# Cross-attention reads and a max-of-three FFN: eight single PSUM banks, turned scores for two batches, and a new order

## The chip, the cores and the metric

The kernel runs on one core of one Trainium2 chip. The metric is device time in microseconds (us), the median of the runs. The engines are TensorE (PE, with its weight loads PEld), VectorE (DVE), ScalarE (ACT), GpSimd (POOL) and SyncE (SP); each works through its own queue in order.

## The reference

`x` is 8 x 8 x 512 x 64 (batch, head, token, depth), `state` 8 x 8 x 32 x 64. Both read each other by attention, and the result goes, per token, through a network whose hidden layer is the largest of three products.

```python
scores = scale * np.matmul(x, state.transpose(0, 1, 3, 2))
a = np.exp(scores - scores.max(-1, keepdims=True)); a /= a.sum(-1, keepdims=True) + 1e-09
xread = np.matmul(a, state)
scores2 = scale * np.matmul(state, x.transpose(0, 1, 3, 2))
a2 = np.exp(scores2 - scores2.max(-1, keepdims=True)); a2 /= a2.sum(-1, keepdims=True) + 1e-09
sread = np.matmul(a2, x)
x = np.concatenate([xread, sread], axis=2)      # then (B*S', H*D) = 4352 x 512
h = np.maximum(np.maximum(x @ w1, x @ w2), x @ w3)
out = h @ w_out                                  # 512 -> 768 -> 512
```

## The kernel before

The exponentials are taken without subtracting the maximum; the sums are looked at near the end, and a branch repeats the work with the maximum if they are out of bounds (it is not taken here). `xread` is never formed: since `xread @ w` is `a @ (state @ w)`, the kernel computes G = state x w for each batch and uses it as the weights of layer 1.

Work is written as a list of short steps, `PLAN`, and each engine's queue holds its instructions in the order of that list; no scheduler moves them. Two further tables give each step its PSUM bank (`BANKS`, and `PAIRS` for tiles of two banks) and its SBUF buffer (`PLACES`). The steps, with b a batch and m one of six blocks of 128 hidden columns:

- `lst`, `lxu`, `lxg`, `lx`, `lw`, `lwo`: loads of state, x, the three weights and w_out. `clr`, `ident`, `zero`, `warm`: constants. `busy`: a PE product nobody uses, which keeps PE working while it waits for data.
- `stc`, `stt`, `stp` k: states of batches 2k and 2k+1 are cast, turned on PE (L261) and placed in a block-diagonal tile `bd`. `xt`/`xtc`: x is turned on PE and copied out (batches 0, 1); `xtd`: turned by DMA from SP.
- `sc` b (PE, L305): scores, x being the standing operand and `bd` the moving one; `ex` (ACT, L313): exponentials e; `sum` (DVE, L342): their sums and reciprocals; `wt` (POOL or DVE, L349): a = e / sum; `at`/`atc` (PE and a copy) or `atd` (DMA from SP): aT. Letters at the end of a step name the engine: A, D, P, S.
- `pad` (POOL, L375): x with a column of ones, so that `sr` (PE, L391) gives the second read with its sum; `srs`, `srt`, `ap` scale it, turn it by DMA and place it. Batches 0 and 1 have no padded x: their `sr` reads 64 columns of x and 64 ones.
- `g` b m, `gr`, `gq` b c0 c1 (PE, L427): G, on eight 64x32 tiles of the array at once; `gc`, `grc`, `gqc` copy it out of PSUM (L444, L466, L469).
- `l1` b m (PE, L477): three products of 512 columns with two passes each, into three banks; `m0` (ACT, L492), `ma`, `mb` (DVE, L497, L505): the largest of the three, ht. `l1s` m: the same for the second reads of all batches. `l2` b j, `l2p` (PE, L514, L532), `l2c`, `l2pc`, `so`, `sop`: layer 2, copies and stores.
- `hold`: one last PE product and a DVE copy of it, ahead of the branch.

Before, PSUM is four single banks and two pairs. A pair takes the G products of both head parities or the scores of a batch, and one instruction then copies both banks:

```python
p = open_ps["g", b, m] = two_banks([128, 2, 512], F32, "pg")
...
copier[c[g]](out=G[b][:, g:h, :, m * 128:m * 128 + 128], in_=p[:, g:h, 0:384]...)
```

The plan begins with batches 0 and 1 together; from batch 2 on each batch repeats one pattern.

Of the kernel before, what the change touches and what calls it, by code (L numbers as in the profile page):

```python
# [18 lines left out]
    lst 0 A; lxu 0 0 S; zero; clr 0; clr 1; clr 2; clr 3; warm; lxg 0 1; busy 1; xones 1; ident; busy 1;  # L19
    lxg 1 0; busy 1; busy 1; stc 0 D; busy 1; busy 1; busy 1; busy 1; busy 1; lxg 1 1; stt 0; busy 1; busy 1;  # L20
    cxu 0 0 D; xt 0 0; stp 0 A; busy 1; xt 0 1; lw 0 2 1; lw 0 1 0; xtc 0 0 D; sc 0 0; xones 0; lw 0 2 2;
    xtc 0 1 D; busy 1; busy 1; sc 0 1; xt 1 0; ex 0 0; ex 0 1; lw 1 3 0; sum 0 0; sum 0 1; xtc 1 0 A; busy 1;
    busy 1; xt 1 1; sc 1 0; xtc 1 1 D; ex 1 0; busy 1; busy 1; sc 1 1; lw 2 3 2; wt 0 1 D; lw 2 3 1; lw 3 4 0;
    wt 0 0 P; lw 3 6 2; at 0 0; sr 0; ex 1 1; sr 1; g 0 0; sum 1 0; wt 1 0 P; g 1 0; atc 0 0 A; at 0 1; at 1 0;
    gc 0 0 A; atc 0 1 A; g 1 1; sum 1 1; gc 1 0 D; atc 1 0 A; srs 0; srs 1; g 0 1; wt 1 1 P; at 1 1; gc 0 1 A;
    l1 0 0; atc 1 1 D; lst 1 A; m0 0 0; lst 3 A; gc 1 1 A; ma 0 0; lw 3 6 1; lw 4 6 0; lxg 2 1; lxg 2 0; l1 0 1;
    m0 0 1; lwo; mb 0 0; g 0 2; g 1 2; ma 0 1; l1 1 0; lst 2 A; gc 0 2 A; mb 0 1; m0 1 0; ma 1 0; l1 0 2;
    mb 1 0; gc 1 2 A; m0 0 2; ma 0 2; l1 1 1; m0 1 1; g 1 3; stc 1 P; mb 0 2; ma 1 1; g 0 3; mb 1 1; stt 1;
    gc 1 3 A; l1 1 2; gc 0 3 A; m0 1 2; stp 1 DA; ma 1 2; g 0 4; g 0 5; l1 0 3; gc 0 5 D; g 1 4; mb 1 2;
    gc 0 4 A; m0 0 3; gc 1 4 A; ma 0 3; gr 2 1792 2304; mb 0 3; l1 1 3; m0 1 3; grc 2 1792 2304 A; xtd 2;  # L30
    ma 1 3; l1 0 5; stc 2 P; g 1 5; gr 2 0 512; mb 1 3; m0 0 5; ma 0 5; l1 1 4; gc 1 5 A; gr 2 1280 1792;
    m0 1 4; grc 2 0 512 D; mb 0 5; gr 2 512 1024; ma 1 4; grc 2 1280 1792 AD; l1 0 4; m0 0 4; ma 0 4; stt 2;
# [45 lines left out]
BANKS = """  # L78
    0123012301 2230210020 1121020310 2321302130 1203102301 2310213012 3120132132 3102301230 2301203103 2103120132
    1032103210 3213201321 0312013201 3201320120 3120132103 1203120312 0310321031 2013210321 0321032132 0132103120  # L80
    1320132103 2103120120 1201320123 0123120123 0213012013 0130123102 2
"""
PAIRS = """
    0101010101 1001010010 0110101010 1010101010 10
"""
PLACES = """
# [657 lines left out]
```

## Time and profile before

| | us |
|---|---|
| median of 3 runs (152.44 to 152.64) | 152.61 |
| span of the profiled execution, first to last instruction | 150.5 |
| median less span | 2.1 |
| PE busy | 145.1 |
| DVE busy | 118.0 |
| ACT busy | 83.2 |
| POOL busy | 56.1 |

The profile is of one execution. The page gives its span; its whole time is not on the page, so the 2.1 us are the distance from the span to the median of the timed runs. "busy" counts instructions of an engine; matmuls are pipelined, so their durations overlap, and the time a group takes on PE is read from the chain in order of time, not from the mean of one.

### The profile page before, as it was taken

What the parts mean: (1) busy time and instruction counts of PE and PEld (TensorE: products, weight loads), DVE (VectorE), ACT (ScalarE), POOL (GpSimd) and SP (SyncE); (2) the same over time, 40 slices, a digit from 0 to 9 for tenths busy, and PEclk for the clock granted to TensorE, in tenths of its full rate; (3) what the DMA queues carried; (4) which work ended last, traced back from release to release, by engine and by line L of the source; (5) the groups of instructions that cost most, each with busy time, mean ns of one, the idle gap of its engine ahead of it and who ended that gap; (6) DMA issues with size and microseconds to landing.
All of it is one profiled execution on the core that took longest, in us unless ns stands there. A gap on an engine that the chain in (4) does not pass through costs nothing.

```text
span 150.5 us, 3618 instructions
## 1 busy us (share of the span) xinstructions
PE 145.1 (96%) x1422; PEld 72.8 (48%) x1422; DVE 118.0 (78%) x202; ACT 83.2 (55%) x144; POOL 56.1 (37%) x78
## 2 busy tenths in 40 slices
PE   6998999999999999999999999999999999999991
PEld 2556443335444443444344434443444446689770
DVE  6488788999967899789978997899789888674443
ACT  3366888965654574457546764676466653332220
POOL 6996911090392507350735064506250200001500
PEclk9999999999999999999999999999999999999999
DMA  4999999949647996998399839983303340300555
GB/s 121 195 188 189 206 230 198 196 97 139 124 97 171 235 182 189 108 209 178 145 102 216 183 139 90 231 183 131 157 4 78 121 175 7 139 0 17 190 199 167
DMA packets 39108, 22.29 MB, mean 148 GB/s; under 512 B 23072, under 2 KB 36896, under 8 KB 39088
## 3 DMA queue, kind: packets, MB, share of 16 engines
q0 software_dynamic: 15872, 13.96, 49.3%
q1 hardware_dynamic: 21632, 6.69, 22.8%
q10 hardware_dynamic: 1584, 1.38, 3.2%
q8 instruction: 12, 0.20, 0.6%
q14 instruction: 8, 0.07, 0.2%
HBM read 15.20 MB, written 8.91 MB: 160 GB/s over the span
## 4 chain that ended last, share of the span: by engine, by line
PE 88%; DMA 5%; POOL 3%; issue 1%; DVE 1%; ACT 1%; POOLq 0%
PE pw L477 47%; PE po L514 25%; PE pg L427 6%; DMA w<-in_moe_w_dram 5%; PE po L532 4%; PE ps L305 2%; PE psr L391 2%; POOL w L217 1%; POOL x L206 1%; PE pgh L427 1%; ACT G L444 1%; PE pt L261 1%; DVE held L593 0%; PE idle L591 0%; PE pat L358 0%
## 5 line engine op out<-in xcount | busy, mean ns | idle before, releaser
L477 PE MATMUL pw<-aT,G 128*128 128x512 bf16 x288 | 66.7, 379 | 0.0
L492 ACT CAST t<-pw 128x512 bf16<-128x512 f32 (+1 forms) x54 | 30.5, 564 | 27.3 <-PE pw L477 26.4
L497 DVE TENSOR_TENSOR t<-t,pw 128x512 bf16<-128x512 bf16 (+1 forms) x54 | 35.3, 654 | 11.1 <-ACT t L492 8.9
L477 PEld LDWEIGHTS <-G 128*128 128x128 bf16 x288 | 27.1, 98 | 32.8 <-issue 2.1
L514 PE MATMUL po<-wout,ht 128*128 128x512 bf16 x168 | 39.7, 379 | 0.0
L505 DVE TENSOR_TENSOR ht<-t,pw 128x512 bf16<-128x512 bf16 x48 | 32.9, 686 | 4.5
L349 POOL TENSOR_TENSOR a<-e,rden 128x1024 bf16<-128x1024 bf16 (+1 forms) x9 | 14.6, 1622 | 27.2 <-ACT osb L526 11.1
L514 PEld LDWEIGHTS <-ht 128*128 128x128 bf16 x168 | 15.4, 98 | 19.0 <-issue 1.7
L548 POOL DMA_DIRECT2D out_dram<-osb x13 | 7.4, 571 | 27.5 <-ACT t L492 27.5
L466 ACT CAST G<-pg 128x1024 bf16<-128x1024 f32 (+1 forms) x17 | 14.7, 895 | 2.1 <-PE pg L427 2.1
L526 ACT COPY osb<-po 128x512 f32<-128x512 f32 x15 | 8.9, 592 | 9.1 <-PE po L514 9.1
L526 DVE COPY osb<-po 128x512 f32<-128x512 f32 x14 | 9.6, 688 | 3.9 <-PE po L514 3.8
L375 POOL COPY xp<-x 128x1024 bf16<-128x1024 bf16 x12 | 12.3, 1059 | 0.0
L313 ACT ACTIVATE e<-ps 128x1024 bf16<-128x1024 f32 (+1 forms) x10 | 8.5, 854 | 6.7 <-PE ps L305 6.7
L466 DVE CAST G<-pg 128x1024 bf16<-128x1024 f32 (+1 forms) x12 | 11.6, 995 | 0.0
L342 DVE TENSOR_REDUCE seen<-e 128x32 f32<-128x1024 bf16 (+1 forms) x10 | 10.0, 997 | 1.7 <-ACT e L313 1.7
L427 PE MATMUL pg<-w,bd 64*32 64x512 bf16 (+1 forms) x288 | 10.7, 362 | 0.4 <-DMA w<-in_moe_w_dram 0.2
L444 ACT CAST G<-pg 128x768 bf16<-128x768 f32 x10 | 8.0, 810 | 2.7 <-PE pg L427 2.5
L543 POOL DMA_DIRECT2D out_dram<-osb x4 | 2.2, 544 | 19.4 <-ACT osb L537 19.4
L249 PE MATMUL idle<-zero 128*128 128x512 bf16 x18 | 7.4, 506 | 1.8 <-DVE zero L225 1.3
L477 PE MATMUL pw<-atp,w 128*128 128x256 bf16 x72 | 8.7, 272 | 0.0
L217 POOL DMA_DIRECT2D w<-in_moe_w_dram x10 | 7.7, 782 | 0.0
(70 smaller groups left out, 112.1 us busy)
## 6 DMA issues: line engine op xcount, KB each, us to landing
out_dram<-osb POOLq DMA_DIRECT2D x12, 512.0 KB, 3.7
x<-in_x_dram POOLq DMA_DIRECT2D x4, 512.0 KB, 7.2
x<-in_x_dram POOLq DMA_DIRECT2D x7, 256.0 KB, 5.8
w<-in_moe_w_dram POOLq DMA_DIRECT2D x4, 256.0 KB, 7.5
w<-in_moe_w_dram POOLq DMA_DIRECT2D x2, 384.0 KB, 7.5
wout<-in_moe_w_out_dram POOLq DMA_DIRECT2D x1, 768.0 KB, 12.0
out_dram<-osb SPq DMA_DIRECT2D x3, 256.0 KB, 2.4
stf<-in_state_dram ACTq DMA_DIRECT2D x4, 128.0 KB, 5.3
```

What stands on the lines that cost most here:

```text
L342: nc.vector.reduce_sum(out=den, in_=parity(e[b], g), axis=AX.X)
L349: times[c](out=parity(a[b], g).rearrange("p j g s n -> p j (g s) n"), in0=parity(e[b], g).rearrange("p j g s n -> p j (g s) n"), in1=rdens ...
L375: nc.gpsimd.tensor_copy(out=xp[b][:, :, :, g * (D + 1):g * (D + 1) + D], in_=v[:, g])
L427: nc.tensor.matmul(p(s, g), bd(b, 2 * s + g)[64 * g:64 * g + 64, g, :], f(w_sb[64 * g:64 * g + 64, s]), start=True, stop=True, tile_positi ...
L444: copier[c[g]](out=G[b][:, g:h, :, m * 128:m * 128 + 128], in_=p[:, g:h, 0:384].rearrange("p g (i f) -> p g i f", i=3))
L466: copier[c[g]](out=v[:, g:h], in_=p[:, g:h, 0:c1 - c0])
L477: nc.tensor.matmul(pw[i][:, 0:n], lhs(i, k), rhs(k), start=(k == 0), stop=(k == nk - 1))
L492: nc.scalar.copy(out=t0s[b, m][:, 0:n], in_=open_ps["l", b, m][0][:, 0:n])
L497: nc.vector.tensor_max(t1s[b, m][:, 0:n], t0s.pop((b, m))[:, 0:n], open_ps["l", b, m][1][:, 0:n])
L505: nc.vector.tensor_max(ht[b][:, m, :], t1s.pop((b, m))[:, 0:n], open_ps.pop(("l", b, m))[2][:, 0:n])
L514: nc.tensor.matmul(p, ht[b][:, m, tokens(b, j)], wout_sb[:, m, :], start=(m == 0), stop=(m == NM - 1))
L526: copier[c[i]](out=o[:, j, i * w:i * w + w], in_=p[:, i * w:i * w + w])
```

## The change

PSUM is eight single banks. The scores, the turned scores and G take two banks each, and every exponential or copy of two banks becomes two instructions, one for each bank; `gq` falls away. `pad` now also serves batches 0 and 1 (on DVE for 0 and 3, else on POOL), with an even row step. Scores of batches 4 and 6 use `sq`, `eq`, `etd`: the states stand, x moves, the exponentials come out turned and a DMA turns them back. States 4 to 7 are turned by DMA (`std`, then `stp` on POOL). All three tables are new.

```diff
     def scores(b, g=None):
+        if g is None:
+            ps = [bank([128, 2, 2, HS, Ns], F32, "ps") for _ in range(2)]
...
     def exps(b, g=None):
-        nc.scalar.activation(
-            out=parity(e[b], g).rearrange("p (c i) g s n -> p i c (g s n)", i=2),
...
+        if g is None:
+            for i in range(2):
+                nc.scalar.activation(
+                    out=out[:, i], in_=ps[i].rearrange("p c g s n -> p c (g s n)"), func=AF.Exp, scale=scale)
...
     def scores_turned(b):
-        p = open_ps["sq", b] = two_banks([128, 2, 2, 2, 128], F32, "pst")
+        ps = open_ps["sq", b] = [bank([128, 2, 2, 128], F32, "pst") for _ in range(2)]
         for g in range(2):
             for s in range(HS):
                 for c in range(2):
                     nc.tensor.matmul(
-                        p[32 * s:32 * s + 32, c, :, g, :], bd(b, 2 * s + g)[64 * c:64 * c + 64, c, :],
+                        ps[c][32 * s:32 * s + 32, :, g, :], bd(b, 2 * s + g)[64 * c:64 * c + 64, c, :],
                         xT[b][64 * c:64 * c + 64, 2 * s + g, :, :],
...
-    def pad(b):
+    def pad(b, c="P"):
...
         for g in range(2):
-            nc.gpsimd.tensor_copy(out=xp[b][:, :, :, g * (D + 1):g * (D + 1) + D], in_=v[:, g])
+            copier[c](out=xp[b][:, :, :, g * (D + 2):g * (D + 2) + D], in_=v[:, g])
...
     def g_slice(b, m):
-        p = open_ps["g", b, m] = two_banks([128, 2, 512], F32, "pg")
+        ps = open_ps["g", b, m] = [bank([128, 512], F32, "pg") for _ in range(2)]
...
     def g_sliced(b, m, c):
...
-        for g, h in ((0, 2),) if len(c) == 1 else ((0, 1), (1, 2)):
...
+        for g, p in enumerate(open_ps.pop(("g", b, m))):
+            copier[c[g % len(c)]](out=G[b][:, g, :, m * 128:m * 128 + 128],
+                                  in_=p[:, 0:384].rearrange("p (i f) -> p i f", i=3))
```

Of the plan, the first line before and after, and the line with the first turned scores:

```diff
-    lst 0 A; lxu 0 0 S; zero; clr 0; clr 1; clr 2; clr 3; warm; lxg 0 1; busy 1; xones 1; ident; busy 1;
+    lxu 0 0 S; lst 0 A; ident; lxg 0 1; zero; clr 2; busy 1; busy 1; busy 1; busy 1; clr 0; busy 1; busy 1; clr
...
+    2; l1 2 4; l2c 1 2 A; m0 2 4; atd 3; ma 2 3; ma 2 5; mb 2 5; mb 2 3; ma 2 4; mb 2 4; gr 4 1792 2304; sq 4;
+    eq 4; l1 2 2; l1 3 4; m0 2 2; ma 2 2; mb 2 2; m0 3 4; grc 4 1792 2304 A; ma 3 4; l1 3 0; so 1 2 4 S; etd 4;
```

The order of the weight loads on POOL was `lw 0 2 1; lw 0 1 0; lw 0 2 2; lw 1 3 0` (columns from and to in blocks of 128, then which weight) and is `lw 0 1 0; lw 0 2 1; lw 0 3 2; lw 1 2 0`.

DVE's queue in the head, from the cast of x 0 to the weights of batch 0, before (`xT` is turned x, `seen` the sums, `a` the weights):

```order
L214 CAST x_82<-osb 128x4x256
L286 COPY xT<-pxt 128x4x256 x2
L342 TENSOR_REDUCE seen<-e 128x4x4
L344 RECIPROCAL rden<-seen 128x16
L342 TENSOR_REDUCE seen<-e 128x4x4
L344 RECIPROCAL rden<-seen 128x16
L286 COPY xT<-pxt 128x4x256
L349 TENSOR_TENSOR a<-e,rden 128x4x128
```

The same place after:

```order
L210 CAST x_82<-osb 128x4x256
L279 COPY xT<-pxt 128x4x256
L376 MEMSET xp 128x16x2
L379 COPY xp<-x_82 128x16x64 x2
L232 MEMSET bd_79 128x512
L346 TENSOR_REDUCE seen<-e 128x4x4
L348 RECIPROCAL rden<-seen 128x16
L346 TENSOR_REDUCE seen<-e 128x4x4
L348 RECIPROCAL rden<-seen 128x16
L353 TENSOR_TENSOR a<-e,rden 128x4x128 x2
```

Two of the three copies of turned x have gone to ACT; the padding of batch 0, the clearing of one `bd` and a second weights step have come in.

ACT's queue in the same stretch, from the placed states to the first G copy, before:

```order
L271 COPY bd_78<-pt 64x16x32 x2
L313 ACTIVATE e<-ps 128x2x2x128 x2
L286 COPY xT<-pxt 128x4x256
L313 ACTIVATE e<-ps 128x2x2x128 x2
L362 COPY aT<-pat 128x4x128
L444 CAST G<-pg 128x6x128
```

and after:

```order
L264 COPY bd_78<-pt 64x16x32 x2
L279 COPY xT<-pxt 128x4x256
L318 ACTIVATE e<-ps 128x2x2x128 x2
L279 COPY xT<-pxt 128x4x256 x2
L318 ACTIVATE e<-ps 128x2x2x128 x2
L366 COPY aT<-pat 128x4x128
L186 DMA stf_75<-in_state_dram 128x256
L366 COPY aT<-pat 128x4x128
L436 CAST G<-pg 128x3x128 x4
```

A copy of turned x now stands ahead of the first exponentials, and G leaves in one instruction for each bank.

DVE's queue around the sums of batch 2 (`sum 2` is the 128x32 reduce), before; the last three rows ahead of the sums place states, cast states and end a max:

```order
L497 TENSOR_TENSOR t_708<-t_706,pw_698 128x512
L505 TENSOR_TENSOR ht<-t_708,pw_699 128x512
L466 CAST G<-pg 128x2x512
L271 COPY bd_80<-pt 64x16x32
L256 CAST st<-stf_77 128x512
L505 TENSOR_TENSOR ht<-t_693,pw_663 128x512
L342 TENSOR_REDUCE seen<-e 128x32
L344 RECIPROCAL rden<-seen 128x32
L497 TENSOR_TENSOR t_811<-t_802,pw_788 128x512
L505 TENSOR_TENSOR ht<-t_811,pw_789 128x512
```

and after:

```order
L476 TENSOR_TENSOR t_750<-t_748,pw_735 128x512
L484 TENSOR_TENSOR ht<-t_744,pw_725 128x512
L448 CAST G<-pg 128x512
L346 TENSOR_REDUCE seen<-e 128x32
L348 RECIPROCAL rden<-seen 128x32
L505 COPY osb<-po 128x512
L484 TENSOR_TENSOR ht<-t_750,pw_736 128x512
L476 TENSOR_TENSOR t_853<-t_847,pw_821 128x512
L484 TENSOR_TENSOR ht<-t_853,pw_822 128x512
```

The state steps have left DVE, the G cast is half as wide, and the last maxima of batch 1 (`mb 1 4`, `ma 1 5`, `mb 1 5`) now come after the sums and an output copy.

More of the change, by code (lines that the diff above doesn't have):

```diff
@@ L686 @@
                 a_turned(b, g, c)
[L687 to L688 removed]
+            pad(b)
             sread_below_max(b)
```

268 lines of the change are left out of this document (119 added, 149 removed), and 4 rows, old and new, of the table BANKS.

## The prediction

> **What bounds the kernel now.** I read the page first (busy shares, then the chain that ended last), then the table by stretch of time, then the chain in order of time, and last the groups by shape for the prices.
>
> ```profile
> PE 145.1 (96%) x1422; PEld 72.8 (48%) x1422; DVE 118.0 (78%) x202; ACT 83.2 (55%) x144; POOL 56.1 (37%) x78
> PE 88%; DMA 5%; POOL 3%; issue 1%; DVE 1%; ACT 1%; POOLq 0%
> ```
>
> TensorE (PE) is busy 145.1 of 150.5 us and carries 88% of the chain. Stretch by stretch (busy us, with the count in brackets; then granted clock, DMA share, GB/s):
>
> ```profile
> core 0: us, PE busy (x) PEld busy (x) DVE busy (x) ACT busy (x) POOL busy (x), PEclk, DMA share, GB/s
> 0.00:13.60 13.60, 11.57 (x154) 6.47 (x155) 9.34 (x19) 6.44 (x10) 10.88 (x21) 1.00 1.16 172
> 13.60:34.30 20.70, 20.50 (x221) 8.53 (x222) 18.18 (x31) 16.45 (x26) 10.35 (x16) 1.00 1.20 182
> 49.30:64.50 15.20, 15.20 (x149) 6.77 (x150) 12.87 (x21) 8.63 (x15) 6.04 (x7) 1.00 0.95 181
> 137.00:147.30 10.30, 9.94 (x99) 7.86 (x97) 5.06 (x14) 2.19 (x7) 2.42 (x5) 1.00 0.49 170
> ```
>
> From 13.6 us on PE has no idle time worth naming; one batch in the middle takes 15.2 us, all of it PE. VectorE (DVE) has 12.9 us of work in those 15.2 and ScalarE (ACT) 8.6, so both have room there. The tight stretch is 13.6 to 34.3, where DVE works 18.2 of 20.7 us and ACT 16.5. So only three things can move the end: PE work taken away, a later or earlier first layer-1 product, and a new wait of PE. The chain in order of time (start, us, what) gives the sizes:
>
> ```profile
> 6.06 7.41 DMA w<-in_moe_w_dram
> 34.06 0.22 PE pt L261 x4
> 34.29 0.47 PE ps L305 x16
> 38.64 0.22 PE pt L261 x4
> 42.75 0.23 PE pgh L427 x8
> 42.98 0.43 PE pg L427 x16
> 43.41 0.38 PE psr L391 x25
> 49.30 5.30 PE pw L477 x24
> 54.60 1.29 PE po L514 x6
> 146.98 0.30 DVE osb L537
> 147.32 0.39 PE idle L591
> 147.74 0.69 DVE held L593
> ```
>
> A unit of layer 1 or layer 2 (six 512-wide products) is 1.29 us. A full score pass (`sc`) is 0.47, a turn of states (`stt`) 0.22.
>
> **The change part by part, on PE.**
>
> States 4 to 7: the two `stt` at 34.06 and 38.64 leave PE, -0.44 us. Exact, since PE has no gap there.
>
> Scores of batches 4 and 6: 16 matmuls of 64 columns (0.47) become 16 of 256 columns on eight 64x32 tiles. Nearest rows: 16 tile matmuls of 512 columns took 0.43, which makes 0.22 for half the columns; eight of 256 columns at the start of a tile stretch took 0.23, which makes 0.46 for sixteen. I take 0.22, because `sq 4` follows `gr 4 1792` and `sq 6` stands ahead of `gr 6`, so no stretch of its own begins. Gain 0.25 each, -0.50 for two; ends -0.02 and -0.50.
>
> Tile stretches: going from full-array products to tiles and back costs time. Going in: 0.23 against 0.11 (a quarter of 0.43) for 256 columns, so 0.12; coming out: 5.30 us for four units against 4 x 1.29 = 5.16, so 0.14. After the first stretch there were 17 of them and now 18: +0.26, ends 0 and +0.5.
>
> The eighteen keep-busy products become 28 and `sr` of batches 0, 1 shrinks from 128 to 65 columns; all of that lies ahead of the first G product, where PE waits anyhow, and is counted with the head.
>
> PE in all: -0.44 - 0.50 + 0.26 = **-0.68 us**.
>
> How long a single such product is shown (mean ns of one):
>
> ```profile
> L427 PE MATMUL pgh<-w,bd 64*32 64x256 bf16 x48 | 1.8, 280 | 0.0
> ```
>
> The Trainium skill, page "TensorE: Matmul & The Clock Gate", section "Part 3: Packing small matmuls" (its paragraph on the span model) says that a pack of n tiles spans one matmul's duration plus about 4 ns for each further tile. By that rule two packs of eight, in series, take 2 x (0.28 + 0.03) = 0.62 us, more than the score pass they replace, and PE would come out at about +0.1 instead of -0.68. The trace does not bear it out as a price in a stream: sixteen of twice the width took 0.43.
>
> **The head** (start, us, engine, instruction, what it waited for):
>
> ```profile
> 1.28 4.02 PE L249 MATMUL idle<-zero 128*128 128x512 bf16 x9 [1.28 <-DVE zero L225]
> 4.95 0.73 DVE L214 CAST x<-osb 128x1024 bf16<-128x1024 f32 x1 [0.91 <-DMA osb<-in_x_dram]
> 5.97 0.65 PEld L278 LDWEIGHTS <-x 128*128 128x128 bf16 x8 [0.34 <-DVE x L214]
> 6.18 0.61 PE L278 MATMUL pxt<-ident,x 128*128 128x128 bf16 x8
> 15.72 2.75 PE L477 MATMUL pw<-aT,G 128*128 128x512 bf16 x12
> ```
>
> Now 14 keep-busy products instead of 11 stand ahead of `xt 0 0`. Cold ones take 0.45 (4.02/9), later ones 0.22 (a sixth of 1.29). Three more at 0.22 make 0.66, less the 0.34 that PE waited there: `xt 0 0` comes 0.3 later (ends 0 and 1.0). From its eviction on, ACT is the long engine: three turned x halves, four exponentials, two turned a halves and G 0 0 in two pieces; its prices stand here (busy us, mean ns of one, idle before):
>
> ```profile
> L466 ACT CAST G<-pg 128x1024 bf16<-128x1024 f32 x12 | 11.7, 1024 | 0.0
> L444 ACT CAST G<-pg 128x768 bf16<-128x768 f32 x10 | 8.0, 810 | 2.7 <-PE pg L427 2.5
> L469 ACT CAST G<-pgh 128x256 bf16<-128x256 f32 x12 | 3.9, 375 | 3.8 <-PE pgh L427 3.8
> L313 ACT ACTIVATE e<-ps 128x1024 bf16<-128x1024 f32 x6 | 6.1, 1025 | 4.2 <-PE ps L305 4.2
> L313 ACT ACTIVATE e<-ps 128x512 bf16<-128x512 f32 x4 | 2.4, 597 | 2.5 <-PE ps L305 2.5
> L526 ACT COPY osb<-po 128x512 f32<-128x512 f32 x15 | 8.9, 592 | 9.1 <-PE po L514 9.1
> L286 ACT COPY xT<-pxt 128x1024 bf16<-128x1024 bf16 x1 | 1.0, 1012 | 0.0
> L286 DVE COPY xT<-pxt 128x1024 bf16<-128x1024 bf16 x3 | 2.1, 691 | 1.5 <-PE pxt L278 1.4
> L375 POOL COPY xp<-x 128x1024 bf16<-128x1024 bf16 x12 | 12.3, 1059 | 0.0
> ```
>
> It can begin when `xt 0 1` is through: 6.18 + 0.61 + 0.3 = 7.1 for `xt 0 0`, then two keep-busy products (0.43) and 0.61, so 8.1, with a handover 8.3. 3 x 1.01 + 4 x 0.60 + 2 x 0.59 (the 592 row) + 2 x 0.48 (between the 375 and 592 rows) = 7.6 us bring it to 15.9, with a few tenths for further handovers to 16.2. Before, l1 0 0 started at 15.72. The weights do not decide: g 0 0 now needs 128 columns (128 KB) more ahead of it, 0.7 us at the 182 GB/s of the table, so 6.06 + 7.41 = 13.47 becomes 14.2; g 0 1 needs the same volume as before. `pad 0 D` is new on DVE ahead of the sums: two copies of 1024 between 0.35 (half the 691 row) and 1.06 (POOL's row), taken at 0.7; it lies where DVE waits for the exponentials. `pad 1 P` (2 x 1.06) follows seven weight loads on POOL and has until the exponentials of batch 1 end, near 13. Head: between 15.9 and 16.2, I take **+0.3 us**, ends -0.2 and +0.7.
>
> **What is to stay hidden.** Each eviction of two banks becomes two: ACT's G casts go from 12 x 1024, 10 x 768, 5 x 512, 12 x 256 columns (27.8 us by these rows, 0.59 for 512) to 34 x 512, 19 x 384, 7 x 256 (31.8), +4; exponentials 12 x 0.60 in place of 6 x 1.02, +1; six more `po` copies +3.6, taken off DVE; two more turned x halves +2, state steps and read copies -2. ACT goes to some 92 us (61%). The cover is 15.2 - 8.6 = 6.6 us per middle batch, of which this takes 1.1; with the cover gone each piece would cost up to 0.16 us (2 x 592 against 1024). DVE's sum stays near 118: less output copies, more `wt` and `pad`. Batch 0's stores go to the end, where the DMA share is 0.49 (1.20 in the head).
>
> POOL gets `stp 2` and `stp 3` (four copies, 0.5 to 1.1 each by its 1059 row). `stp 2` stands behind `wt 3`: `sc 2` starts at about 36 (34.29, the head's 0.3, one unit of layer 2 now ahead of it), `sc 3` at 46.5 (the 9.4 us worked out below and a unit), its weights are done 5.4 later, so `stp 2` by 55; `gr 4 1792`, which needs it, comes at 56. Zero, and one for one if it is later. `lx 4` stands behind `wt 2` on POOL, at 41.5 or so. Its load and the turn on SP land in the median in
>
> ```profile
> x<-in_x_dram POOLq DMA_DIRECT2D x4, 512.0 KB, 7.2
> xT<-x SPq DMA_TRANSPOSE x6, 5.3
> ```
>
> and so by 54.0; `sq 4` follows `gr 4 1792` at 56.2. Zero, with 2 us to spare.
>
> Batches 4 and 6 get a longer chain: `sq`, two exponentials, a DMA turn, then `sr`. `sq 4` to `sr 4` is five units and two runs, 7.0 us; the chain is 0.2 + 1.2 + 3.2 (the slowest turn of a, below) = 4.6, queued on SP behind the issue of one store. That store starts some 2.7 us before the turn, about what its 512 KB take at 182 GB/s (2.8). Zero; if it went fully first, 0.4.
>
> **Tail.** `hold` waited for the last DVE copy (146.98, then 147.32) since its bank was the last one used; now its bank is that of `l2 s 1`, long free: -0.3 on that chain. The last store still follows the last copy on ACT. I take **-0.1**, ends 0 and -0.3.
>
> Sum: -0.68 + 0.3 - 0.1 = -0.5 us: span 150.0 against 150.5. The timed median is 152.61, 2.1 above the span, which I carry over: **152.1 us**. A difference under 0.2% (0.3 us) is about what a measurement of this kernel cannot tell from none.
>
> **Rivals.**
>
> Slower, a wait at batch 2. Its chain before, and the landing of a's turns by DMA:
>
> ```profile
> 34.85 1.02 ACT L313 ACTIVATE e<-ps 128x1024 bf16<-128x1024 f32 x1 [1.03 <-PE ps L305]
> 38.29 1.21 DVE L342 TENSOR_REDUCE seen<-e 128x32 f32<-128x1024 bf16 x1
> 40.04 1.91 POOL L349 TENSOR_TENSOR a<-e,rden 128x1024 bf16<-128x1024 bf16 x1 [6.10 <-ACT t L492]
> DMA to landing us min/median/max: 2.7/2.9/3.2
> ```
>
> The new order leaves fewer units between `sc 2` and l1 2 0: 0.47 + 5 x 1.29 + one tile stretch (0.23 + 0.43 + 0.38 + 0.14) + 1.29 = 9.4 us. The chain from the start of `sc 2`: 0.56 + 1.2 (two half exponentials) to the sum, 1.75 to POOL's start (38.29 to 40.04), 1.91, 2.9 = 8.3 us. So l1 2 0 waits as soon as `sum 2` starts later than 2.8 us after `sc 2`. Before it started 4.0 after (38.29 - 34.29); the same lag would give 4.0 + 1.75 + 1.91 + 2.9 = 10.6, a wait of 1.2 us, and 153.3. For it: DVE is nearly full in this stretch, and gets `wt 0 0` and `pad 0` in the head; the same lag would also hold l2 1 0, which needs `mb 1 5` the fourth DVE instruction after the sums. Against: what stood between in DVE's queue (a 1024 G cast, a state copy and cast, one max) is gone from there. Chance 0.22.
>
> No change, the head eats it: if the three keep-busy products run cold and handovers add up, l1 0 0 starts at 16.5 rather than 16.0 and the tail gives nothing: -0.68 + 0.7 = 0.0, 152.6. For it: ACT's 7.6 us have no slack. Against: the 0.34 wait was there to be filled. Chance 0.20.
>
> The turned scores save nothing: two eights that do not overlap, each 0.28 + 0.03, make 0.62 for 0.47. Then PE is -0.44 + 0.30 + 0.26 = +0.12 and the sum +0.3: 152.9. The 0.43 for sixteen speaks against. Chance 0.04.
>
> (That rival is the span model of the Trainium skill's page "TensorE: Matmul & The Clock Gate" taken as a price.)
>
> Some other wait on the new DMA turns or on the two output buffers that batches 1 to 7 now share: 153.5 or more, chance 0.03.
>
> **How the numbers follow.** The forecast, 152.1, has 0.51; its own range, with the ends of the terms, is 151.3 to 152.5, so 0.05 of it lies within 0.2%. Faster: 0.46. Same: 0.05 + 0.20 = 0.25. Slower: 0.22 + 0.04 + 0.03 = 0.29. The range from 151.1 to 153.5 takes in every end but the last rival and the far tail of the wait at batch 2.
>
> **What would show it.** In the profile after: no `pt` at 34 or 38; the turned scores in 0.2 to 0.25 us on PE; first `pw` product at 16.0 +- 0.3; PE without waits from there; ACT near 92 us; `hold` right behind the last `po`. I am wrong if PE waits for a DMA of `aT` or `e` or for DVE's `ht` in the stretch from 36 to 47 us, or if the first `pw` starts before 15.5 or after 16.6.

## The result: 160.25 us, and where the 7.9 us went

The changed kernel takes 160.25 us (median) against 152.31 for the kernel before in the same session: ratio 1.050, 95% interval 1.046 to 1.054. Forecast were 152.1, with a range to 153.5. Two of its six runs, 162.3 and 163.3 us, lie over 1.5% above the fastest and are left out of the ratio, though not of the median.

The page of the changed kernel, engines and chain:

```profile
PE 146.6 (92%) x1408; PEld 72.9 (46%) x1424; DVE 114.4 (72%) x211; ACT 87.4 (55%) x176; POOL 52.6 (33%) x72
PE 55%; DMA 18%; POOL 11%; issue 6%; ACT 4%; DVE 3%; POOLq 0%; DVEq 0%
```

TensorE's work grew only from 145.1 to 146.6 us, but its share of the chain fell from 88% to 55%: 18% is now DMA and 11% GpSimd. So PE waits (5.2 us for DMA, below). To see where, I cut both traces at the same points of the program: the first layer-1 product, the start of `sr 2`, the start of `sr 3`, and the held product at the end (columns as in the table by stretch of the prediction; the third from the right is the granted clock, the share of TensorE's full clock). The changed kernel:

```profile
0.00:16.12 16.12, 14.63 (x203) 7.70 (x205) 11.03 (x26) 9.75 (x16) 12.33 (x22) 1.00 1.17 174
16.12:45.00 28.88, 27.34 (x252) 11.40 (x246) 23.17 (x39) 19.82 (x43) 14.24 (x19) 1.00 1.17 156
45.00:55.05 10.05, 7.29 (x98) 3.34 (x92) 5.55 (x12) 4.61 (x10) 0.31 (x1) 0.83 0.97 130
55.05:153.83 98.78, 96.99 (x879) 50.43 (x884) 73.76 (x135) 52.98 (x110) 25.71 (x32) 1.00 0.61 141
153.83:158.90 5.07, 0.38 (x4) 0.04 (x1) 0.85 (x2) 0.27 (x1) 0.00 (x0) 0.75 0.35 105
```

and the kernel before:

```profile
0.00:15.72 15.72, 13.49 (x198) 7.58 (x199) 10.93 (x24) 8.13 (x14) 13.01 (x23) 1.00 1.24 174
15.72:43.34 27.62, 27.62 (x253) 11.58 (x250) 23.87 (x36) 20.42 (x35) 11.53 (x18) 1.00 1.02 161
43.34:48.85 5.51, 5.51 (x99) 2.71 (x92) 4.42 (x8) 3.08 (x7) 2.64 (x4) 1.00 0.74 163
48.85:147.32 98.47, 98.09 (x891) 50.88 (x884) 78.08 (x136) 51.61 (x94) 28.95 (x35) 1.00 0.62 140
147.32:150.50 3.18, 0.38 (x1) 0.00 (x0) 0.69 (x1) 0.00 (x0) 0.00 (x0) 1.00 0.41 125
```

The difference by stretch: +0.40 in the head, +1.26 up to `sr 2`, +4.54 from `sr 2` to `sr 3`, +0.31 from there to the held product, +1.89 at the end; together the 8.4 us between the spans. In the stretch of 4.54, PE was busy 7.29 of 10.05 us where it had been busy 5.51 of 5.51, and the granted clock was 0.83. What it waited for (us in total, times, longest) and the pieces of the chain:

```profile
PE pw L456 <- DMA aT<-a: 3.9, 2, 2.7
PE ps L303 <- DMA xT<-x: 1.3, 1, 1.3
```

```profile
22.07 6.11 DMA x<-in_x_dram
28.20 9.05 DMA xT<-x
42.54 6.98 DMA aT<-a
73.32 7.04 DMA aT<-a
154.25 0.69 DVE held L572
```

Three DMA turns are late: xT of batch 2 took 9.05 us, aT of batches 2 and 4 took 7.0 each. In the kernel before the slowest turn of an xT landed after 6.0 us, of an aT after 3.2. The queues at the second of them (start, us, engine, line, instruction):

```profile
40.61 1.91 POOL L353 TENSOR_TENSOR a<-e,rden 128x1024 bf16<-128x1024 bf16 x1 [7.46 <-DVE rden L348]
42.47 0.95 POOL L197 DMA_DIRECT2D x<-in_x_dram  x1
```

GpSimd finishes `wt 2` at 42.5, and in that instant SyncE issues the turn (42.54) and GpSimd, next in its own queue, the 512 KB load `lx 4` (42.47). In the kernel before, `lx 4` stood behind a pad and a store and left at 44.54, 2.6 us after its turn, with the turn nearly landed.

### The profile page after: what moved, and what is told of

Same layout as the page of the kernel before. It is cut to its first block, busy times and chain, and to the rows that moved or that the text cites. A ratio compares the mean times of both kernels' runs of the same rounds, so it can differ in the third digit from the quotient of the medians.

```text
span 158.9 us, 3619 instructions
## 1 busy us (share of the span) xinstructions
PE 146.6 (92%) x1408; PEld 72.9 (46%) x1424; DVE 114.4 (72%) x211; ACT 87.4 (55%) x176; POOL 52.6 (33%) x72
## 4 chain that ended last, share of the span: by engine, by line
PE 55%; DMA 18%; POOL 11%; issue 6%; ACT 4%; DVE 3%; POOLq 0%; DVEq 0%
PE pw L456 26%; PE po L493 14%; DMA aT<-a 9%; DMA xT<-x 6%; POOL a L353 4%; PE idle L242 4%; PE po L511 4%; DMA x<-in_x_dram 4%; POOL bd L264 3%; POOL w L213 2%; PE pg L420 2%; DVE seen L346 2%; PE ps L303 2%; ACT e L315 1%; POOL xp L379 1%
## 5 line engine op out<-in xcount | busy, mean ns | idle before, releaser
L353 POOL TENSOR_TENSOR a<-e,rden 128x1024 bf16<-128x1024 bf16 (+1 forms) x6 | 9.7, 1621 | 46.8 <-DVE rden L348 44.4
L448 ACT CAST G<-pg 128x512 bf16<-128x512 f32 (+1 forms) x41 | 20.5, 564 | 6.0 <-PE pg L420 6.0
L505 ACT COPY osb<-po 128x512 f32<-128x512 f32 x21 | 12.4, 595 | 10.4 <-PE po L493 10.2
L448 DVE CAST G<-pg 128x512 bf16<-128x512 f32 (+1 forms) x19 | 11.0, 611 | 2.5 <-PE pg L420 2.5
L420 PE MATMUL pg<-w,bd 64*32 64x512 bf16 (+2 forms) x336 | 11.6, 350 | 0.1
L527 POOL DMA_DIRECT2D out_dram<-osb x4 | 2.3, 566 | 22.3 <-ACT osb L505 22.3
L436 ACT CAST G<-pg 128x384 bf16<-128x384 f32 x19 | 8.1, 492 | 1.0 <-PE pg L420 0.8
L456 PEld LDWEIGHTS <-w 128*128 128x128 bf16 x72 | 6.9, 98 | 1.0
L315 ACT ACTIVATE e<-ps 128x512 bf16<-128x512 f32 x8 | 4.3, 594 | 4.9 <-PE ps L303 4.9
L505 DVE COPY osb<-po 128x512 f32<-128x512 f32 x8 | 5.5, 687 | 1.9 <-PE po L493 1.8
```

What stands on the lines that cost most here:

```text
L353: times[c](out=parity(a[b], g).rearrange("p j g s n -> p j (g s) n"), in0=parity(e[b], g).rearrange("p j g s n -> p j (g s) n"), in1=rdens ...
L420: nc.tensor.matmul(p(s, g), bd(b, 2 * s + g)[64 * g:64 * g + 64, g, :], f(w_sb[64 * g:64 * g + 64, s]), start=True, stop=True, tile_positi ...
L448: copier[c[g % len(c)]](out=v[:, g, c0:c1], in_=p[:, 0:c1 - c0])
L456: nc.tensor.matmul(pw[i][:, 0:n], lhs(i, k), rhs(k), start=(k == 0), stop=(k == nk - 1))
L505: copier[c[i]](out=o[:, j, i * w:i * w + w], in_=p[:, i * w:i * w + w])
```

## The experiments

Two theories at the start. Theory 1: a load that leaves beside a DMA turn makes the turn late, and PE waits for it. Theory 2: SyncE's queue itself is slow, since it has more turns (states 4 to 7 and e of batches 4 and 6: 24 blocks of 128 x 128 more). Beside these: the stores at the end, and the narrower weight loads.

**r1, two loads held back.** A copy of one element of aT stands ahead of the load on GpSimd.

```diff
-    atd 2; ... lx 4; ...
+    atd 2; ... gate 2; lx 4; std 2; ...
-    wt 4 - P; lx 6; ... pad 5 P; lx 7
+    wt 4 - P; ... pad 5 P; gate 4; lx 6; lx 7
+    def see_turn(b):
+        last = work.tile([128, 1], BF16, tag="last", bufs=1, name="last")
+        nc.gpsimd.tensor_copy(out=last, in_=aT[b][:, 0, 0, 0:1])
```

> The changed kernel, with only the loads of x of batches 4 and 6 issued later: GpSimd first copies one element of aT of batch 2 (of batch 4), so that the load leaves after that turn has landed. Theory 1 (a DMA turn takes 7 us instead of 2.7 when a load of x from GpSimd's queue leaves in the same instant, and TensorE waits for it): the turns of aT of batches 2 and 4 take 2.7 to 3.5 us, the first layer of batch 2 waits under 0.5 us instead of 2.7, that of batch 4 not at all, and the slow-clock stretch behind the first goes: 160.25 - (2.7 + 1.2 + up to 2.0) = 154.5 to 157. Theory 2 (the turns are slow for what stands on SyncE's own queue, the state turn behind aT's, or because there are more DMA turns): both still take about 7 us, and the time stays at 159.5 to 160.8.

159.03 us (1.048 of before, 1.040 to 1.056). How the turns of aT landed over the whole run, and two pieces of the chain:

```profile
DMA to landing us min/median/max: 3.0/3.1/7.2
```

```profile
26.20 11.21 DMA xT<-x
55.33 7.16 DMA aT<-a
```

The two turns whose loads were held back went to about 3 us, as theory 1 has it; the turn of batch 3, whose load `lx 5` still left beside it, now showed at 7.16, and xT of batch 2 took 11.2. The mechanism held and the sum did not (154.5 to 157 were expected): the wait moved on.

**r2, batch 0 stored early.**

```diff
-    so 0 0 2 A; ... so 0 2 4 P
+    xtd 4; so 0 0 4 S
```

> The changed kernel, with batch 0's 1 MB of output stored in one transfer from SyncE right behind the turn of xT of batch 4 (about 53 us) and no longer at the end. Theory 1 (the end of the span is set by a pile of stores, which ends 4.0 us after the last vector operation where the kernel before has 2.07): 1 to 2 us less, 158.2 to 159.3, with the stretch from that operation to the end at 2.0 to 2.8 us. Theory 2 (the last stores take as long without the pile): 159.8 to 160.7. A new cost would be the turn of aT of batch 3, about 57 us, beside the store: up to 4 us longer, and TensorE waiting for it.

160.93 us, and the span still ended 4.1 us after the held operation. Storing batch 0 early gained nothing, which fits the prediction's zero for its stores at the end.

**r3, the second half of batch 2's x ahead of the weights.**

```diff
-    lw 4 5 0; lw 4 5 2; ... stc 1 P; ... lxg 2 0
+    lxg 2 0; lw 4 5 0; lw 4 5 2; ... stc 1 P
```

> The changed kernel, with the second half of batch 2's x loaded about 5 us earlier, ahead of the six weight loads on GpSimd's queue instead of behind them and behind the cast of states. Theory 1 (TensorE waits 1.3 us ahead of the scores of batch 2 because this load leaves at 22.1 us and the turn behind it ends at 37.2): the turn ends by 34, the scores do not wait, -1.3 us or more, 158.0 to 159.0, unless the wait for aT behind it grows by what was saved: that turn then begins earlier too, so it should not. Theory 2 (the weights that now come 0.8 us later are waited for, or the turn stays long for the loads beside it): 160 to 161.

164.68 us (1.079, 1.072 to 1.087): theory 2 of that pair, and more than its range. The turn came earlier, and the load of `w_out` beside it took 15.3 us to land in place of 9.3, in a profiled run of 166.04 us. That the slowing goes both ways is better seen in r13 below.

**r4, the kernel before with one load beside the turn.**

```diff
-    wt 2 - P; ... so 0 0 2 P; lx 4
+    wt 2 - P; lx 4; ... so 0 0 2 P
```

> The kernel before, with one load moved: that of batch 4's x stands right behind batch 2's weights on GpSimd (as in the changed kernel) and not two steps later, so that it leaves in the same instant as the turn of aT of batch 2. Theory 1 (load beside turn): that turn takes about 7 us instead of 2.7, TensorE waits 3 to 4 us ahead of batch 2's first layer and then runs up to 2 us slowly: 155.5 to 158.5. Theory 2 (the queue of SyncE or the larger number of DMA turns in the changed kernel makes them slow, not the load): within 0.5 us of 152.6.

158.34 us, 1.044 of before (1.035 to 1.052). One moved load costs 6.2 us. The landing of its aT turns, and PE's wait:

```profile
DMA to landing us min/median/max: 2.7/2.8/8.4
```

```profile
PE pw L473 <- DMA aT<-a: 4.7, 1, 4.7
```

One turn of six took 8.4 us, all others 2.7 to 3.0; PE waited 4.7 us, then ran the next 5.4 us at a clock of 0.71. Nothing else of the change is in this kernel, so for batch 2 the moved load is shown to be enough. The size is not the load's alone: this kernel's two 512 KB stores left at 44.55, 2.9 us behind the turn, when an undisturbed one would have landed.

**r7, a store beside the turn.**

```diff
-    wt 2 - P; ... so 0 0 2 P; lx 4; ... so 0 2 4 P
+    wt 2 - P; so 0 0 1 P; so 0 3 4 P; ... lx 4; ... so 0 1 3 P
```

> The kernel before, with 512 KB of batch 0's output (two transfers of 256 KB) stored from GpSimd's queue in the instant in which the turn of aT of batch 2 leaves, where the load of batch 4 stood in the run of the kernel before with a load beside; that load stands behind them, at its old time. Theory 1 (what harms a turn is a load of x, which casts from float32 on its way): the turn takes 2.7 to 3.5 us and the time is within 0.4 us of 152.2. Rival (any half megabyte beside it does): the turn takes 5 us or more, TensorE waits 1 to 4 us, 154 to 158.

157.77 us (1.038, 1.035 to 1.041): the rival, in part. The turn took 5.9 us and PE waited 2.3:

```profile
DMA to landing us min/median/max: 2.7/2.9/5.9
```

So a turn is late beside stores too, without a load of x and its cast leaving in the same instant. How much the stores alone cost is open, since the load `lx 4` left at 45.42, 3.1 us behind the turn and before it had landed. Most of the rest of the 5.7 us is no wait for a DMA:

```profile
SPq L735 <- DVEq L670: 3.1, 1, 3.1
```

At the end SyncE waited 3.1 us for VectorE's queue at the branch, 0.4 in the run r4, and the span ended 4.3 us after the held operation. The programs of VectorE and ScalarE are one instruction longer here, and the instruction queue moved three packets in the end stretch, not two; that a fetch is the cause is argued from the trace and was not tried apart.

**r5 and r6, more loads held back.** Batch 3's loads wait for xT of batch 2, that of batch 5 for aT of batch 3; r6 also moves three of batch 6's stores to GpSimd.

```diff
-    pad 2 P; lxg 3 1; ... ones; ... lxg 3 0
+    pad 2 P; ... ones; gate xT 2; lxg 3 1; lxg 3 0
-    lx 5; stp 2 P; ... pad 4 P
+    stp 2 P; ... pad 4 P; gate aT 3; lx 5
```

> The changed kernel, with every load of x that left beside a turn held back in the same way: those of batch 3 until xT of batch 2 has landed, of 4, 5 and 6 until aT of batch 2, 3 and 4 has. In the run that held back two of them, TensorE still waited 2.0 us for xT of batch 2 (a turn of 11.2 us, with a load of batch 3 beside it) and 1.2 us for aT of batch 3 (7.2 us, with the load of batch 5), and ran slowly for some 1.7 us after the first. Theory 1 (a load that leaves beside a turn is the cause of every long turn): xT of batch 2 turns in 5 to 6 us, each aT in 2.7 to 3.5, TensorE waits under 0.5 us in all between 30 and 90 us, the span is 152 to 153.5 and the time 153.7 to 155.3. Theory 2 (the turn of xT of batch 2 is long for the load of wout, which is still beside it, and there are simply more turns): it stays over 8 us, and the time within 0.7 of 158.4.

> As the run with all turns clear, and three of batch 6's stores at the end (1 MB in all) go over GpSimd's queue and not SyncE's. In the changed kernel SyncE's queue moves 1.7 MB in the last 14 us, against 0.66 MB before, and one trickle of it is still moving 1.5 us after all others. Theory 1 (the queue's share is what ends late): the span ends 2.0 to 2.5 us after the last vector operation and not 4.0, 1.5 to 2.0 us less than the run with clear turns. Theory 2 (the bytes at the end set it, whatever their queue; storing batch 0 early did not help either): the same time as that run within 0.4 us.

162.67 and 161.64 us: worse, where theory 1 of r5 had 153.7 to 155.3. Two things show in the chain of r5:

```profile
26.85 9.59 DMA xT<-x
42.39 1.91 SPq L283
44.35 4.91 DMA aT<-a
```

The turn of xT of batch 2 still took 9.59 us, so batch 3's loads were not what made it long; `w_out` was still beside it, as theory 2 of r5 had it. And batch 3's x came so late that its turn left right ahead of aT of batch 2, on the same in-order queue. A turn behind a turn is late as well: 4.91 us here. The end was 4.2 us in r6: the queue of batch 6's stores has no part in it.

**r8, r9, r10, wide and narrow weights.** r8 and r9: r5's holds and

```diff
-    lw 4 5 0; lw 4 5 2; lw 5 6 0; lw 5 6 1; ... lw 5 6 2; ... lw 4 5 1
+    lw 4 6 0; lw 4 6 2; lw 4 6 1
```

with 16 more instructions of ScalarE (r8) or VectorE (r9) in the branch not taken. r10: the kernel before, `lw 3 6 2`, `lw 3 6 1` and `lw 4 6 0` in pieces of 128 columns.

> The changed kernel with all loads of x held back as in the run with all turns clear, and the six weight loads of 128 columns behind the first layer's start made three of 256 columns, so that GpSimd issues three fewer and the loads behind them leave some 2.3 us earlier. In the trace of the changed kernel the 16 DMA engines are fully busy from 16 to 32 us, yet move about 150 GB/s from 19 us on, where the kernel before moves 200 with wider pieces. Theory 1 (narrow pieces make the loads late; with the turns clear and the loads on time nothing is waited for): xT of batch 2 has landed by 34 us, the waits of TensorE between 30 and 90 us come to under 0.7 us, and the last vector operation stands at 147.5 to 148.5 (147.7 before). Theory 2 (the turns are slow for another reason): it stays at 151 or later. Besides, the branch that is never taken is made longer by 16 ScalarE instructions, which moves the end of that engine's program. Theory of the end (an instruction fetch that one engine's end needs once more than before; 3 packets of the instruction queue there, not 2): if that engine is ScalarE, the span ends 2.1 us after the last vector operation and not 4.1. If it is the stores: 4.1.

> The same kernel, with the never-taken branch made longer by 16 VectorE instructions in place of ScalarE's. Up to the last vector operation it should repeat that run within 0.5 us. The end: if it is VectorE's program that needs one more fetch, the span ends 2.1 us after that operation; if ScalarE's, another engine's, or the stores, 4.1.

> The kernel before, with its three last weight loads (two of 384 columns and one of 256) cut into pieces of 128 columns, in place; all else as it was, so GpSimd issues five more loads. Theory 1 (narrow pieces lower the rate of the loads and make batch 2 late): the loads move about 150 to 165 GB/s in 16 to 28 us and not 200, xT of batch 2 lands some 3 us later, TensorE waits 1 to 2 us ahead of batch 2's scores: 153.5 to 156.5. Theory 2 (the width doesn't matter; only the place of the loads does): within 0.5 us of 152.1.

158.80, 159.96 and 152.33 us. In r10 the width did nothing (1.000, 0.998 to 1.003), and its loads moved almost as much, 204 GB/s between 20 and 28 us against 212; theory 1 fell there (in the profiled run xT of batch 2 made PE wait 0.9 us, and the median does not show it). In r8 xT of batch 2 landed in time (32.9 us), which fits three issues fewer on GpSimd (2.3 us); the narrow pieces cost by their issues, if at all. But the waits moved again, from r8's chain:

```profile
41.46 5.35 DMA aT<-a
53.30 6.07 DMA xT<-x
61.00 7.37 DMA e<-eT
```

The held load of batch 5 had left at 60.55, beside the new turn of e of batch 4. The longer programs left the end at 3.9 us in both. r9 came 1.2 us later than r8 and not within 0.5: its chain holds a load of states (4.16 us, ahead of the cast that batch 2's turn follows) which r8's does not.

**r11, the branch held 0.9 us longer.**

```diff
-    hold; vl
+    busy 4; hold; vl
```

> The changed kernel, with four more idle products of TensorE (0.9 us) ahead of the one that holds the branches back at the end; nothing else. In the changed kernel the end of the span waits 1.4 us for a last packet trickle of a store, which goes on for 0.9 us after the instruction fetches of the branch, 0.6 us after the bulk of the stores is through; in the kernel before the stores are through 0.2 us after the held operation and the fetch comes behind them. Theory 1 (the fetch overtakes the last stores on one DMA engine): with the branch 0.9 us later the trickle is gone, the span ends 2.1 us after the held operation and not 4.0, and the time is 0.8 to 1.1 us less: 159.0 to 159.5. Theory 2 (one engine's program takes the long fetch whatever is in flight, or that last store is late by itself): the tail stays 4.0 or falls to 3.1, and the time is 160.2 to 161.2.

161.25 us; the end fell only from 4.0 to 3.4 us after the held operation, and the time did not fall. Theory 1 of that run fell as it stood.

**r12, r13, no loads of x for batches 2 to 7.**

```diff
+    for b in range(2, B):
+        x_sb[b] = x_sb[b - 2]
```

and the steps `lx` and `lxg` of these batches dropped, so the outputs of batches 2 to 7 are not theirs.

> The changed kernel without the loads of x of batches 2 to 7: these read the tiles of batches 0 and 1 in their place (so their outputs are those of other batches; every instruction but the eleven loads' remains). Theory 1 (turns are late because loads of x share the DMA engines with them, and come late themselves): TensorE waits for no turn for more than 0.3 us, its clock does not fall, and with the same head and tail the time is 160.25 - (1.3 + 2.7 + 1.2 of waits and about 2 of slow clock) = 152.5 to 154.0. Theory 2 (the changed kernel simply has more turns, 24 blocks of 128 x 128 more, and they queue behind each other on SyncE): turns of aT still take 5 us or more and the time is above 156.

> The kernel before without the same loads, batches 2 to 7 reading the tiles of batches 0 and 1. It waits for no turn as it is, so both theories expect no more than 0.6 us less: 151.5 to 152.3. Against it the changed kernel without loads shows what the change would be worth if no load stood beside a turn: the prediction's terms give -0.7 on TensorE, +0.4 at the head, and 2.0 at the end.

159.66 us for the changed kernel and 161.77 for the one before, both far above what was expected (152.5 to 154.0 by theory 1, 151.5 to 152.3). Above 156, as theory 2 has r12, it is for another reason. Without a load to wait for, SyncE issued the turns of x of batches 2 and 3 from 7.1 us on, beside the weights, and now the weights were late; PE waited for them 3.8 us in r12 and 7.8 in r13. From r13's chain:

```profile
15.72 16.46 DMA w<-in_moe_w_dram
```

Loads of the weights, which landed in 8.4 us at most in the kernel before, took 16.5 beside these turns, and `w_out` 20.3 in place of 12.0. So the slowing goes both ways. Past that stretch the two runs are clean, and they give the number that was looked for, `sr 2` to `sr 3` to the held product in r12:

```profile
49.44:54.94 5.50, 5.45 (x97) 2.71 (x90) 4.59 (x11) 4.50 (x10) 0.00 (x0) 1.00 0.93 123
54.94:152.51 97.57, 96.94 (x879) 50.52 (x884) 74.33 (x137) 52.91 (x110) 23.30 (x29) 1.00 0.44 127
```

```profile
DMA to landing us min/median/max: 3.0/3.1/3.2
```

5.50 + 97.57 = 103.07 us, where the kernel before takes 103.98 both with its loads (43.34 to 147.32) and without (54.24 to 158.22). All 24 added blocks are still in r12, and its turns of aT land in 3.0 to 3.2 us. The kernel before, without loads, has 2.7 to 2.8. Whether the added turns cost the others these 0.3 us is not shown: the next run has none of them, and its quickest aT still takes 3.1. As the cause of the 4 us more, theory 2 is out.

**r14, the added turns undone.**

```diff
-    std 2; ... stp 2 P; ... std 3; ... stp 3 P
+    stt 2; stp 2 A; ... stt 3; stp 3 A
-    sq 4; eq 4; ... etd 4;     sq 6; eq 6; ... etd 6
+    sc 4 -; ex 4 -;            sc 6 -; ex 6 -
```

> The changed kernel with all its added DMA turns undone: the states 4 to 7 are turned by TensorE again (two bursts of four, 0.22 us each, placed by ScalarE) and the scores of batches 4 and 6 are made standing as for the others, so the four turns of e and states are gone from SyncE's queue; orders and loads are the changed kernel's. Theory 1 (loads and the place they leave from): the turns of xT and aT of batch 2 take 9 and 7 us as before, the waits of 1.3, 2.7 and 1.2 us stay, and the time is 160.0 to 161.5 (TensorE has 0.9 us more). Rival (the added turns are what makes DMA slow): the turns of aT take 3 to 4 us, 155 to 157.5.

162.35 us, with the same long turns (one aT piece of its chain):

```profile
42.49 6.53 DMA aT<-a
```

Theory 1 by its mechanism; the time came out 0.9 above its range, since PE also waited twice 0.9 us for the placing on ScalarE.

**r15, the loads paced.** Wide weights; batch 3's loads behind the landing of `w_out`; 4 and 5 together behind aT of batch 2; 6 and 7 behind aT of batch 4.

```diff
-    pad 2 P; lxg 3 1; ... ones; ... lxg 3 0
+    pad 2 P; ... ones; lxg 3 1; lxg 3 0
-    lx 4; ... lx 5; ... lx 6; ... lx 7
+    gate aT 2; lx 4; lx 5; ... gate aT 4; lx 6; lx 7
```

> The changed kernel with its loads paced, the rest untouched: the six late weight loads are three wide ones; both loads of batch 3's x stand behind the landing of wout, and so leave near 30.5 us and not at 28.2 beside batch 2's turn; those of batches 4 and 5 leave together when aT of batch 2 has landed, those of 6 and 7 when aT of batch 4 has. From the run without loads, the stretch from the read of states of batch 2 to the last operation of TensorE takes 103.1 us if no turn is waited for (104.0 in the kernel before, 108.8 in the changed one); from the runs with wide weights, that read can begin by 43.0 to 43.6 us. Theory 1 (loads that leave beside a turn, and that alone): 43.3 + 103.1 to 104.0 = 146.4 to 147.3 for that last operation, and with the end as it is (5.1 us) a time of 153.2 to 154.5. Theory 2 (waits only move to the next turn, whatever the pace, since the DMA engines are full): 149 or later, 156 to 159.

155.14 us (1.018, 1.014 to 1.021), 3.1 above the kernel before in its session where the changed kernel was 7.9 above: 4.8 us are back with every transfer in place. It is 0.6 above theory 1's range. `sr 2` to the held product takes 104.7 us; one wait is left, for xT of batch 4:

```profile
PE pst L324 <- DMA xT<-x: 1.4, 1, 1.4
```

**r16, other queues for two of the last stores.**

```diff
-    sop 7 2 128 384 S; ... sop 7 1 384 512 S
+    sop 7 1 384 512 A; ... sop 7 2 128 384 P
```

> The same, and two of the last stores leave from other queues than SyncE's, as in the kernel before (one of batch 7 from GpSimd, one from ScalarE). Theory 1 (SyncE's queue, which has three stores to issue in the last 1.7 us, is what ends late): the span ends 2.1 to 2.6 us after the held operation and not 4.0, and the time is 1.5 us less than the paced run's: 151.7 to 153. Theory 2 (a packet of an engine that also fetches instructions, whatever the queue): 4.0, and the same time within 0.4 us.

156.38 us, 1.2 more than r15, and the end at 4.9 us: the queue alone does not do it.

**r17 and r18, the end.** r17 is r15 with the turned scores of batch 4 two tiles later and with the end of the kernel before; r18 puts the held product's bank back.

```diff
-    sq 4; eq 4; l1 2 2; l1 3 4; m0 2 2; ... m0 3 4; grc 4 1792 2304 A
+    l1 2 2; l1 3 4; sq 4; grc 4 1792 2304 A; m0 2 2; ... m0 3 4; eq 4
-    l2pc 7 0 128 256 A; ... sop 7 1 384 512 S; ... hold      (bank 6)
+    l2pc 7 0 128 256 D; ... sop 7 1 384 512 A; ... hold      (bank 0 in r17, 6 in r18)
```

> The paced run with two more edits. The turned scores of batch 4 come two tiles of the first layer later (2.6 us), since the paced run still waited 1.4 us for xT of batch 4 there, and nothing needs them so early. And the end is as in the kernel before: the last eviction is VectorE's and not ScalarE's, one of the last stores leaves ScalarE and not SyncE, and the held product takes the bank of the last eviction, so it waits for it. Theory 1 (the pace, and an end in which stores leave after the branch is let go): no wait of TensorE for a turn over 0.3 us, the stretch from the read of states of batch 2 to the held product 103.0 to 103.5 us, the span ends 2.1 to 2.8 us after the held operation: 151.6 to 153.0. Theory 2 (the wait moves on to e or aT of batch 4, and the end is a property of the whole program): 154.5 to 156.

> The last run with one thing put back: the held product at the end takes bank 6 again, as in the changed kernel, and so waits for nothing; the last eviction and the last stores stay as in the kernel before. The prediction counted the free bank as a gain of up to 0.3 us. Theory 1 (who evicts last and which queue stores last made the end 1.9 us longer): the span ends 2.0 to 2.4 us after the held operation, which comes 0.4 earlier, and the time is that of the last run within 0.5 us, 153.1 to 153.9. Theory 2 (the free bank lets the branch go before the stores are through): the end takes 3.5 to 4.2 us after the held operation, and the time is 154.6 to 155.6.

r17: 153.57 us, 1.0073 of before (1.0052 to 1.0095). r18: 154.90 (1.015, 1.008 to 1.023). r17 lies between its two theories: the end came as theory 1 has it (1.9 us), but `sr 2` to the held product took 105.1 us and not 103.0 to 103.5. r18 is theory 2 of its pair. r17 by the same stretches, without the head:

```profile
16.49:43.83 27.34, 27.14 (x253) 11.54 (x248) 23.16 (x39) 19.84 (x43) 11.20 (x15) 1.00 1.06 164
43.83:49.33 5.50, 5.45 (x97) 2.70 (x90) 4.59 (x11) 4.50 (x10) 2.02 (x3) 1.00 0.65 83
49.33:148.96 99.63, 97.68 (x880) 50.37 (x884) 74.87 (x138) 53.02 (x110) 25.30 (x32) 1.00 0.64 149
148.96:152.00 3.04, 0.37 (x1) 0.00 (x0) 0.69 (x1) 0.00 (x0) 0.00 (x0) 1.00 0.40 116
```

The clock is 1.00 throughout, the stretch up to `sr 2` is 0.28 shorter than before, that to `sr 3` the same, and the end takes 3.04 us from the held product where the kernel before has 3.18. What SyncE waited for at its end, in r17 and then in r18:

```profile
SPq L722 <- DMA out_dram<-osb: 0.4, 1, 0.4
```

```profile
SPq L722 <- DMA out_dram<-osb: 1.7, 1, 1.7
```

One digit of the bank table took the end from 1.9 to 3.9 us after the held operation, in one profile of each; the intervals of the two ratios overlap a little. With bank 0 the held product waits for the last eviction, and the branch comes after it. The other profiles agree: where the held product waits so (before, r4, r7, r10, r13, r17), the last store packet is through 0.3 us after the held operation, and where its bank is free (the other fourteen) 1.7 to 2.7 us. The span ends 1.7 to 2.0 us after that operation in the first group, but 4.3 in r7 for the other wait told above, and 3.4 to 4.9 in the second. In r11 the branch came later by idle products, with the changed kernel's order of evictions and stores, and most of the long end stayed; in r18 the order was that of the kernel before and the wait was missing, and all of it stayed. The waiting bank with the changed kernel's order was not run, so it is open whether the bank alone would do.

What is left of r17's 1.3 us is in its trace the head (+0.8, first layer-1 product at 16.49) and 1.16 us more from `sr 3` on, 0.9 of it PE waiting for aT of two batches. No version here beats the kernel before.

## Why the prediction was wrong, step by step

- **PE terms, -0.68: right in sum.** Up to `sr 2`, 27.34 against 27.62 us (r17): -0.28. From there, with no load beside a turn, 103.07 against 103.98 (r12), of which 0.4 is the held product's wait that the changed kernel does not have: -0.5. In all -0.8, put together from two runs. The turned scores of batch 4 took 0.22 on PE in r5 and r6 but 0.34 to 0.41 in r8, r9 and r15 to r18, those of batch 6 0.34: the gain of 0.25 each was the favourable end of its range. The third rival would have made it 0.62.
- **Head, +0.3: right.** 16.12 against 15.72 (expected 16.0 +- 0.3), though one profile says little about 0.3 us: the same head fell between 15.5 and 16.6 in most of the later ones, and at 18.1 in r2. ScalarE was the long engine in it, as said (8.5 to 16.1); `xt 0 0` came 0.8 later, not 0.3 (6.95 against 6.18), inside its ends.
- **ACT near 92 us:** 87.4, hidden as said. **Batch 0's stores at the end, zero:** storing them early gained nothing (r2). **`stp 2`, zero:** it started at 57.5 and not "by 55"; no wait of PE shows there.
- **"`lx 4` stands behind `wt 2` on POOL ... Zero, with 2 us to spare": the step that failed.** It counted when the load lands for `sq 4` and not what it does to the turn that leaves in the same instant. The chain of batch 2 in the first rival used 2.9 us for the landing of a's turn, the median of a kernel in which the 512 KB load left 2.6 us later; here it was 6.98. The price: 2.7 us of wait and 1.6 to 1.8 of slow clock behind it, all in the +4.54 stretch. The same step for `lx 6` and aT of batch 4: 7.04, a wait of 1.2. There a second term had been put at nothing: `stp 3` stands ahead of `wt 4` on POOL, and `wt 4` began at 71.39, 1.3 after its sums were ready (70.09). Without that the wait would have been gone too, by an estimate from these times.
- **A term that was missing:** xT of batch 2. Its second half is loaded at 22.07 us where the kernel before has issued both halves by 18.1, and the turn took 9.05: `sc 2` waited 1.3. With batch 3's loads held back it still took 9.59 (r5); with the wide weights as well it took 6.5 (r8). Which load beside it made it long was not tried apart.
- **The first rival had the right place and the wrong cause.** It priced a wait at batch 2 at 1.2 by a lag of DVE; `sum 2` started 1.6 us after `sc 2` (38.85, 37.29), under its limit of 2.8, so by its own arithmetic there was no wait. The sign it gave, PE waiting for a DMA of aT behind the stretch from 36 to 47 us, came (46.86 to 49.57).
- **Tail, -0.1: wrong by 2.0.** "`hold` ... now its bank is ... long free: -0.3" was the step. With the bank free the span ended 3.9 us after the held operation, with the bank of the last eviction 1.9 (r18, r17). By what mechanism is open: with a branch that only came later (r11) it was still 3.4.

The clock behind a wait, in the changed kernel and in r11, the same work from the end of the same wait of 2.7 us (the wait left out):

```profile
49.57:55.05 5.48, 5.48 (x53) 2.51 (x54) 3.32 (x6) 2.23 (x5) 0.31 (x1) 0.69 0.62 110
```

```profile
49.40:53.30 3.90, 3.82 (x52) 1.79 (x52) 2.42 (x5) 2.23 (x5) 0.00 (x0) 1.00 0.53 92
```

5.48 us at a granted clock of 0.69 against 3.90 at 1.00. The Trainium skill, page "TensorE: Matmul & The Clock Gate", section "Part 1: The HAM clock gate", says that the clock drops after an idle window of about 3.4 us whose start does not depend on the program; that the same wait costs 1.6 us once and nothing in another run agrees with the second half, while a drop behind a gap of 2.7 us (and in r1 behind one of 2.0, clock 0.73) is shorter than the window it names. In all the traces the drops behind waits go to 0.50 and last 3.41 us (6.8 in r5); the changed kernel's runs from 50.57 to 53.98 us, and so begins 1.0 us after PE is back at work. Waits of 2.0 to 2.7 us brought one in the changed kernel, r1, r2 and r14 and none in r7, r8, r9 and r11.

## What to carry to other kernels

A DMA turn's landing time is not a constant: it was 2.7 to 3.2 us in the kernel before and 5 to 8.4 with half a megabyte or another turn leaving beside it, so for each turn that PE waits for, list what every queue issues from its start until it lands, and price it with the row that has the same company. When loads are moved off one turn, look where they come down: the wait went from batch 2 to 3 to 4 until all loads had a place, and holding a load back can delay the turn that needs it on an in-order queue. A product that seems to wait for nothing useful may be what keeps the end in order; change its bank and read the end again.

## What was not expected of the hardware

- Half a megabyte leaving 0.07 us ahead of a turn of 256 KB made that turn 7.0 us in the changed kernel and 8.4 instead of 2.8 in r4, where two stores followed; stores of the same size, with the load 3.1 us behind, made it 5.9 (r7).
- The slowing is mutual: weights landed in 16.5 us beside turns of x (r13), in 8.4 at most in the kernel before; `w_out` in 20.3 and 12.0.
- One instruction more on VectorE and on ScalarE went with 2.7 us more of SyncE's wait at the final branch (r7 against r4: 3.1 and 0.4), with the same work ahead of it.
- In the changed kernel's long end, all stores but a few packets are through 0.6 us after the held operation; the last 18 packets, of the two queues of SyncE and ScalarE, come 1.5 to 2.2 us after it, behind an instruction fetch that ends at 1.5. That the fetch holds them up on one DMA engine fits this and was not shown.
